# An FFT-mixing kernel's first batch: filter loads held back behind the input, a constant moved to another DMA queue, and filter rows loaded instead of copied

## The chip, the cores and the metric

One core of a Trainium2 chip. The metric is the time of one execution on the device in microseconds (us), lower is better. The kernel before was at 780.32 us (median of three runs, 779.61 to 780.56). The profile's own span leaves out a little at the ends: 778.8 us for that kernel.

## The reference, cut to what matters

```python
# x: (8, 3008, 256); filt_r, filt_i: (1505, 256); w_in: (256, 2048); w_out: (2048, 256)
X = np.fft.rfft(x, axis=1)
F = (filt_r + 1j * filt_i)[None, :, :]
y = np.fft.irfft(X * F, n=3008, axis=1).astype(np.float32)
t = y.reshape(24064, 256)
h = t @ w_in
out = np.maximum(0.01 * h, h) @ w_out
```

The FFT of length 3008 = 94 x 32 is done as matmuls with constant matrices: `small` (the first, 94-point step, and the last, 32-point step of the inverse), `f2` (the second step with its twiddles) and `i1` (the inverse). Between the steps, transposes and products with the filters run on the vector engine.

## The kernel before

Batches 1 to 7 are mixed while the two big matmuls of the batches before them keep TensorE busy. Batch 0 has nothing to hide behind, so it has its own, quicker code, and nothing of the big matmuls starts before it is through. It is done in two halves of 128 channels ("first half", "second half"). The filter tiles `fa_sb` and `fb_sb` need the same rows twice: in partitions 0 to 63 (loaded from DRAM) and again in 64 to 127 ("upper rows", copied).

The loads, as they are issued at the top. All but `small` go through the queue that GpSimd issues to:

```python
def filt_load(dst, src, d0, dn):          # two loads of 192 KB, fp32 in DRAM, fp16 in the tile
    for q, first, sgn in ((0, 0, 1), (Q, N1, -1)):
        nc.gpsimd.dma_start(
            dst[q : q + Q, :, ds(d0, dn)],
            bass.AP(tensor=src.tensor, offset=src.offset + first * D + d0,
                    ap=[[N1 * D, N2 // 2], [sgn * NC * D, 2], [sgn * D, NC], [1, dn]]))

nc.sync.dma_start(small_sb[:], small_d.ap())                 # SyncE's queue
first_parts = ((0, 10), (10, 10), (20, 8), (28, 4))
for n0, nn in first_parts:
    x_load(0, n0, nn)                                        # batch 0 in four parts
for hf in range(2):
    filt_load(fa_sb, filt_r, hf * DH, DH)
    filt_load(fb_sb, filt_i, hf * DH, DH)
    for i in (1, 0, 2) if hf == 0 else ():
        nc.gpsimd.dma_start(f2_sb[:, ts(i, NC // FP), :], f2_d.ap()[i])
nc.gpsimd.dma_start(w_in_sb[:], moe_w_in.rearrange("(dt p) c -> p dt c", p=P))
```

The work of batch 0:

```python
def upper(hf, t, copy):
    copy(t[64:P, :, ts(hf, DH)], t[0:64, :, ts(hf, DH)])

keep_warm(14)                       # matmuls on zeros, to have TensorE at full clock
g = 0
for n0, nn in first_parts:
    while nn:
        n = 2 if nn % 4 or n0 >= N2 - 4 else 4
        first_s1(n0, n, two[n // 4], (dve, act)[g % 2])     # 94-point step, result copied to big
        n0, nn, g = n0 + n, nn - n, g + 1
    keep_warm(5 if n0 < N2 else 14)
t1_part(0, 0, True)(), t1_part(0, 1, True)()                # transposes, first half
upper(0, fa_sb, act), upper(0, fb_sb, dve)                  # upper rows of the first half
first_s2(0, 8, 8, "ph", True)                               # matmuls with f2, products with fa, fb
t1_part(0, 2, True)()
first_s2(0, 0, 8, "ph")

nc.vector.memset(i1_sb[:, 0, 0:2], 0.0)                     # the i1 load waits for this memset
nc.sync.dma_start(i1_sb[:], i1_d.ap())
for n0 in (0, N2 // 2):
    x_load(1, n0, N2 // 2)
t1_part(0, 3, True)()
upper(1, fa_sb, act)                                        # upper rows of the second half
first_s2(0, 16, 4, "pf"), first_s2(0, 20, 4, "pf")
upper(1, fb_sb, dve)
keep_warm(4)
first_s2(1, 0, 8, "ph")
# ... rest of batch 0, then the steady loop over the big matmuls
```

A small memset in front of a load is the kernel's way of holding the load back: the load overwrites what the memset wrote, so it waits for the memset, which stands behind other work in the vector engine's order.

Of the kernel before, what the change touches and what calls it, by code (L numbers as in the profile page):

```python
# [10 lines left out]
P = 128  # L11
# [7 lines left out]
N1, N2 = 94, 32  # L19
NC = 24  # L20
Q = 32
R1 = 96
FP = 3
# [46 lines left out]
def kernel(  # L70
# [9 lines left out]
    nc = tc.nc  # L80
    B, N, D = x.shape
# [11 lines left out]
    f2_d = nc.inline_tensor(f2_np, name="fwd2_const")  # L93
    i1_d = nc.inline_tensor(i1_np, name="inv1_const")
    small_d = nc.inline_tensor(small_np, name="small_const")

    cpool = ctx.enter_context(tc.tile_pool(name="const", bufs=1))
    f2_sb = cpool.tile([P, NC, P], FP16, name="f2_sb")
    i1_sb = cpool.tile([P, N2, N1], FP16, name="i1_sb")
    small_sb = cpool.tile([P, 3, P], FP16, name="small_sb")  # L100
    fa_sb = cpool.tile([P, NC, D], FP16, name="fa_sb")
    fb_sb = cpool.tile([P, NC, D], FP16, name="fb_sb")
    w_in_sb = cpool.tile([P, NDT, DFF], FP16, name="w_in_sb")
    w_out_sb = cpool.tile([P, NCT, D], FP16, name="w_out_sb")
    x_sb = cpool.tile([P, N2, D], FP16, name="x_sb")
# [15 lines left out]
    def bank(kind, n, w):  # L121
        of = wide if kind == "ph" else single
        t = of[turn[kind] % len(of)]
        turn[kind] += 1
        return t[:, : n * w].rearrange("p (n w) -> p n w", n=n)
# [4 lines left out]

    DH = D // 2

    def x_load(b, n0=0, nn=N2, d0=0, dn=D):

        for lo, cnt in ((0, R1),) if b + 1 < B else ((0, 64), (64, N1 - 64)):
            nc.gpsimd.dma_start(  # L136
                x_sb[lo : lo + cnt, ds(n0, nn), ds(d0, dn)],
                bass.AP(tensor=x.tensor, offset=x.offset + (b * N + lo * N2 + n0) * D + d0,
                        ap=[[N2 * D, cnt], [D, nn], [1, dn]]))

    def filt_load(dst, src, d0, dn):

        for q, first, sgn in ((0, 0, 1), (Q, N1, -1)):
            nc.gpsimd.dma_start(
                dst[q : q + Q, :, ds(d0, dn)],
                bass.AP(tensor=src.tensor, offset=src.offset + first * D + d0,
                        ap=[[N1 * D, N2 // 2], [sgn * NC * D, 2], [sgn * D, NC], [1, dn]]))


    nc.sync.dma_start(small_sb[:], small_d.ap())  # L150
    first_parts = ((0, 10), (10, 10), (20, 8), (28, 4))
    for n0, nn in first_parts:
        x_load(0, n0, nn)
    for hf in range(2):
        filt_load(fa_sb, filt_r, hf * DH, DH)
        filt_load(fb_sb, filt_i, hf * DH, DH)
        for i in (1, 0, 2) if hf == 0 else ():
            nc.gpsimd.dma_start(f2_sb[:, ts(i, NC // FP), :], f2_d.ap()[i])
    nc.gpsimd.dma_start(w_in_sb[:], moe_w_in.rearrange("(dt p) c -> p dt c", p=P))
    idle = cpool.tile([P, CH], FP16, name="idle")  # L160
    nc.vector.memset(idle[:], 0.0)

# [18 lines left out]
    def spread(dst, n0, ps, copy, e0=0):  # L181
        nn, de = ps.shape[1], ps.shape[2] // 2
        copy(paired(dst)[:, ds(n0, nn), ds(e0, de)], ps.rearrange("p n (e t) -> p n e t", t=2))  # L183
# [3 lines left out]
    def t1_part(b, i, flat=False):  # L187
        def go():
            a = big[(4 * b) % 3][:].bitcast(FP32)[:, ts(i, E4 * Q)].rearrange("p (e n) -> p e n", n=Q)
            o = big[(4 * b + 1) % 3][:].bitcast(FP32)  # L190
            if flat:
                o = o[:, ts(i, E4 * Q)].rearrange("p (e n) -> p e n", n=Q)
            else:
                o = o.rearrange("p (n e) -> p e n", n=Q)[:, ts(i, E4), :]
            nc.vector.transpose(o, a)  # L195
        return go
# [52 lines left out]
    act, dve = nc.scalar.copy, nc.vector.tensor_copy  # L249

    def first_s1(n0, n, kind, copy):
        ps = bank(kind, n, D)
        for j in range(0, n, 2):
            nc.tensor.matmul(ps[:, ds(j, 2), :], fwd1[:N1], x_sb[:N1, ds(n0 + j, 2), :],  # L254
                             start=True, stop=True)
        spread(big[0], n0, ps, copy)
# [50 lines left out]
        yv = yt[:, dt, :N].rearrange("p (a c) -> p a c", c=N2)  # L307
        copy(yv[:, :, ds(4 * h, 4)], ps.rearrange("p c a -> p a c"))

    def upper(hf, t, copy):  # L310
        copy(t[64:P, :, ts(hf, DH)], t[0:64, :, ts(hf, DH)])


    def keep_warm(n):
        for _ in range(n):
            nc.tensor.matmul(po_ps.rearrange("p a d -> p (a d)"), idle[:, 0:P], idle[:],  # L316
                             start=True, stop=True)

    keep_warm(14)
    g = 0  # L320
    for n0, nn in first_parts:
        while nn:
            n = 2 if nn % 4 or n0 >= N2 - 4 else 4
            first_s1(n0, n, two[n // 4], (dve, act)[g % 2])
            n0, nn, g = n0 + n, nn - n, g + 1
        keep_warm(5 if n0 < N2 else 14)
    t1_part(0, 0, True)(), t1_part(0, 1, True)()
    upper(0, fa_sb, act), upper(0, fb_sb, dve)
    first_s2(0, 8, 8, "ph", True)
    t1_part(0, 2, True)()  # L330
    first_s2(0, 0, 8, "ph")

    nc.vector.memset(i1_sb[:, 0, 0:2], 0.0)
    nc.sync.dma_start(i1_sb[:], i1_d.ap())
    for n0 in (0, N2 // 2):
        x_load(1, n0, N2 // 2)
    t1_part(0, 3, True)()
    upper(1, fa_sb, act)
    first_s2(0, 16, 4, "pf"), first_s2(0, 20, 4, "pf")
    upper(1, fb_sb, dve)  # L340
    keep_warm(4)
    first_s2(1, 0, 8, "ph")
    first_sa(0, 0, 8)
# [87 lines left out]
    for slot in range(SL * (NCHUNK + 1)):  # L431
        ci, g = divmod(slot, SL)
# [36 lines left out]
```

## Time and profile before

| | before |
|---|---|
| device time, median of 3 | 780.32 us |
| span in the profile | 778.8 us |
| TensorE busy | 768.5 us |
| x's first matmul | 7.07 us |
| first transposes of batch 0 on the vector engine | 14.77 us |
| first matmul of the second half | 22.87 us |
| first matmul of the steady loop (L377) | 39.36 us |

TensorE is busy nearly throughout, so the steady loop cannot give or take much; whatever moves the first matmul of L377 moves the end. The prediction below shows the chain of waits and the loads. Two more lines of the timeline of the kernel before belong to its argument (start in us, duration, engine, line, operation, operands, count; in brackets the idle time of the engine just before, and what ended it):

```profile
22.87 1.04 PE L267 MATMUL ph<-big,f_sb 128*128 128x128 f16 x8 [2.01 <-DVE big L195]
...
39.36 1.31 PE L377 MATMUL ph<-yt,w_in_sb 128*128 128x512 f16 x4
```

The first says that TensorE stands still for 2.01 us in front of the second half, because the transpose of L195 on the vector engine is what it waits for. The second is the marker: all before it is front, all after it is the steady loop.

### The profile page before, as it was taken

The numbers are of one execution on the slowest core, as the hardware profiler recorded it, in microseconds if no ns is written. First come the engines' busy times: TensorE is split into PE (matmuls) and PEld (weight loads), VectorE is DVE, ScalarE is ACT, GpSimd is POOL, SyncE is SP. The second block draws the span as 40 slices with busy tenths as digits, with TensorE's granted clock in tenths as the row PEclk, the third lists the DMA queues.
The fourth block names the chain that finished last, engine by engine and source line by source line (L and its number), as shares of the span: only waits on it lengthen the run. The fifth ranks groups of instructions, "written<-read, shape, count | busy, mean of one in ns | idle before, by whom it ended". The sixth has DMA issues, their size and how long they took to land.

```text
span 778.8 us, 13329 instructions
## 1 busy us (share of the span) xinstructions
PE 768.5 (99%) x5688; PEld 521.5 (67%) x5688; DVE 369.6 (47%) x468; ACT 553.5 (71%) x784; POOL 148.7 (19%) x123
## 2 busy tenths in 40 slices
PE   8899999999999999999999999999999999999998
PEld 4556666666776676666777667666667667666666
DVE  5989742765238641576407743187523764200000
ACT  5777768676787768777686775967668676666663
POOL 6854200330005200042002410025000330000000
PEclk9999999999999999999999999999999999999999
DMA  9951013210151010510105010230101010110111
GB/s 186 227 92 56 28 41 71 66 42 29 41 108 42 28 41 28 116 35 28 42 28 122 28 41 29 53 96 28 41 28 42 28 38 31 41 42 28 41 41 55
DMA packets 36154, 43.36 MB, mean 56 GB/s; under 512 B 8130, under 2 KB 34370, under 8 KB 35330
## 3 DMA queue, kind: packets, MB, share of 16 engines
q0 software_dynamic: 10208, 17.01, 12.4%
q1 hardware_dynamic: 25888, 25.52, 9.3%
q8 instruction: 44, 0.72, 0.4%
q14 instruction: 14, 0.11, 0.1%
HBM read 34.10 MB, written 24.64 MB: 75 GB/s over the span
## 4 chain that ended last, share of the span: by engine, by line
PE 96%; DVE 2%; ACT 1%; DMA 1%; issue 0%; DVEq 0%; POOLq 0%
PE ph L377 41%; PE po_ps L391 41%; PE pf L173 3%; PE pf L241 2%; PE pf L213 2%; PE pf L229 2%; PE pf L391 1%; DMA x_sb<-in_x_dram 1%; DVE big L195 1%; DVE prod L281 1%; PE pf L288 0%; ACT big L183 0%; PE po_ps L316 0%; PE ph L267 0%; PE ph L254 0%
## 5 line engine op out<-in xcount | busy, mean ns | idle before, releaser
L382 ACT ACTIVATE gt_c<-ph 128x1024 f16<-128x1024 f32 x376 | 384.9, 1024 | 195.5 <-PE ph L377 193.4
L377 PE MATMUL ph<-yt,w_in_sb 128*128 128x512 f16 (+3 forms) x1600 | 386.6, 367 | 0.3
L391 PE MATMUL po_ps<-w_out_sb,gt_c 128*128 128x256 f16 x2944 | 381.5, 273 | 0.5 <-ACT ost_c_t L398 0.5
L391 PEld LDWEIGHTS <-gt_c 128*128 128x128 f16 x3008 | 290.5, 98 | 82.3 <-issue 2.4
L377 PEld LDWEIGHTS <-w_in_sb 128*128 128x128 f16 x1600 | 154.4, 98 | 97.5 <-issue 0.4
L222 POOL TENSOR_TENSOR y_b_g<-p_b_g,p_b_g 128x512 f16<-128x512 f32 x84 | 106.8, 1272 | 225.7 <-DVE p_b_g L220 225.7
L195 DVE STREAM_TRANSPOSE big<-big 128x1024 f32<-128x1024 f32 x32 | 56.0, 1846 | 126.0 <-ACT big L183 125.9
L183 ACT CAST big<-pf 128x512 f16<-128x512 f32 x186 | 106.6, 605 | 1.1 <-PE pf L254 1.1
L244 DVE CAST yt<-pf 128x376 f16<-128x376 f32 x112 | 56.4, 545 | 86.0 <-PE pf L241 86.0
L218 DVE TENSOR_TENSOR p_b_g<-pf,fa_sb 128x512 f32<-128x512 f32 x84 | 58.1, 692 | 38.3 <-PE pf L213 35.3
L398 ACT COPY ost_c_t<-po_ps 128x256 f32<-128x256 f32 x184 | 69.4, 377 | 6.6 <-PE po_ps L391 5.4
L203 DVE STREAM_TRANSPOSE big<-big 128x1024 f32<-128x1024 f32 x28 | 51.1, 1936 | 34.0 <-ACT big L183 34.0
L219 DVE TENSOR_TENSOR p_b_g<-pf,fb_sb 64x512 f32<-64x512 f32 x84 | 58.2, 692 | 1.1
L220 DVE TENSOR_TENSOR p_b_g<-pf,fb_sb 64x512 f32<-64x512 f32 x84 | 57.4, 683 | 1.1
L136 POOL DMA_DIRECT2D x_sb<-in_x_dram x13 | 7.1, 548 | 253.7 <-PE pf L173 252.9
L241 PEld LDWEIGHTS <-big 128*128 128x128 f16 x448 | 25.7, 98 | 13.2
L173 PE MATMUL pf<-x_sb,small_sb 94*128 94x512 f16 x112 | 33.6, 380 | 0.2 <-DVE yt L244 0.2
L213 PE MATMUL pf<-big,f_sb 128*128 128x256 f16 x168 | 32.1, 273 | 0.0
L229 PE MATMUL pf<-y_b_g,small_sb 128*128 128x512 f16 x84 | 31.9, 380 | 0.0
L213 PEld LDWEIGHTS <-f_sb 128*128 128x128 f16 x168 | 16.4, 98 | 19.7
L241 PE MATMUL pf<-i_sb,big 128*128 128x94 f16 x448 | 28.7, 206 | 0.0
L173 PEld LDWEIGHTS <-small_sb 94*128 94x128 f16 x112 | 10.7, 98 | 10.5
(50 smaller groups left out, 166.8 us busy)
## 6 DMA issues: line engine op xcount, KB each, us to landing
out_dram<-ost_c_t SPq DMA_DIRECT2D x92, 256.0 KB, 2.1
x_sb<-in_x_dram POOLq DMA_DIRECT2D x5, 1536.0 KB, 11.1
x_sb<-in_x_dram POOLq DMA_DIRECT2D x2, 768.0 KB, 12.1
x_sb<-in_x_dram POOLq DMA_DIRECT2D x3, 480.0 KB, 7.3
w_in_sb<-in_moe_w_in_dram POOLq DMA_DIRECT2D x1, 1024.0 KB, 13.3
w_out_sb<-in_moe_w_out_dram POOLq DMA_DIRECT2D x1, 1024.0 KB, 11.8
x_sb<-in_x_dram POOLq DMA_DIRECT2D x1, 1024.0 KB, 8.1
fa_sb<-in_filt_r_dram POOLq DMA_DIRECT2D x4, 192.0 KB, 8.5
```

The costliest lines, as they stand in the source:

```text
L173: nc.tensor.matmul(ps, fwd1[:N1], x_sb[:N1, ds(2 * g, 2), :], start=True, stop=True)
L183: copy(paired(dst)[:, ds(n0, nn), ds(e0, de)], ps.rearrange("p n (e t) -> p n e t", t=2))
L195: nc.vector.transpose(o, a)
L213: nc.tensor.matmul(ps[:, j, :], f2_sb[:, 2 * g + j, :], src[:, 2 * g + j, :], start=True, stop=True)
L218: nc.vector.tensor_tensor(p1[:], ps, fa, AL.mult)
L219: nc.vector.tensor_tensor(p2[0:64], ps[64:P], fb[64:P], AL.mult)
L222: nc.gpsimd.tensor_tensor(y1[:], p1[:], p2[:], AL.add)
L241: nc.tensor.matmul(ps[:, j, :], src[:, dt, n2, :], i1_sb[:, n2, :], start=True, stop=True)
L377: nc.tensor.matmul(ph[:, j, ds(o, ln)], w_in_sb[:, dt, ts(ct, P)], yt[:, dt, ds(lo, ln)], start=(dt == 0), stop=(dt == NDT - 1),)
L382: nc.scalar.activation(gts[ci][:, ds(2 * g, 2), :], ph, AF.Lrelu)
L391: nc.tensor.matmul(po, gts[ci][:, ct, ts(tj, P)], w_out_sb[:, ct, :], start=(ct == 0), stop=(ct == NCT - 1))
L398: nc.scalar.copy(ost[:, tj % 2, :], po)
```

## The change

The intent, as the code shows it: let x come in alone, with the filters held until the first copies of batch 0 are done; take `f2` and most of `small` to SyncE's queue, held a little longer; fetch the upper rows of the second half from DRAM, which takes a copy each from ScalarE and the vector engine; and load `w_in` later. Ten warming matmuls instead of 14 stand in front, as if x were expected earlier.

```diff
-    nc.sync.dma_start(small_sb[:], small_d.ap())
+    nc.sync.dma_start(small_sb[:, 0, :], small_d.ap()[:, 0, :])
     first_parts = ((0, 10), (10, 10), (20, 8), (28, 4))
     for n0, nn in first_parts:
         x_load(0, n0, nn)
-    for hf in range(2):
-        filt_load(fa_sb, filt_r, hf * DH, DH)
-        filt_load(fb_sb, filt_i, hf * DH, DH)
-        for i in (1, 0, 2) if hf == 0 else ():
-            nc.gpsimd.dma_start(f2_sb[:, ts(i, NC // FP), :], f2_d.ap()[i])
-    nc.gpsimd.dma_start(w_in_sb[:], moe_w_in.rearrange("(dt p) c -> p dt c", p=P))
 # ... filt_load gets an argument p0, the first partition to write
-    keep_warm(14)
+    keep_warm(10)
 # ...
             first_s1(n0, n, two[n // 4], (dve, act)[g % 2])
+            if g == 0:
+                nc.vector.memset(fa_sb[0:1, 0, 0:2], 0.0)
+                for hf in range(2):
+                    filt_load(fa_sb, filt_r, hf * DH, DH)
+                    filt_load(fb_sb, filt_i, hf * DH, DH)
+                filt_load(fa_sb, filt_r, DH, DH, 64)
+                filt_load(fb_sb, filt_i, DH, DH, 64)
+            if g == 2:
+                nc.vector.memset(f2_sb[:, 8, 0:2], 0.0)
+                for i in (1, 0, 2):
+                    nc.sync.dma_start(f2_sb[:, ts(i, NC // FP), :], f2_d.ap()[i])
+                nc.sync.dma_start(small_sb[:, 1:3, :], small_d.ap()[:, 1:3, :])
 # ...
     nc.sync.dma_start(i1_sb[:], i1_d.ap())
+    nc.gpsimd.dma_start(w_in_sb[:], moe_w_in.rearrange("(dt p) c -> p dt c", p=P))
 # ...
-    upper(1, fa_sb, act)
     first_s2(0, 16, 4, "pf"), first_s2(0, 20, 4, "pf")
-    upper(1, fb_sb, dve)
```

More of the change, by code (lines that the diff above doesn't have):

```diff
@@ L131, with x_load, filt_load @@
     DH = D // 2
-    def x_load(b, n0=0, nn=N2, d0=0, dn=D):
+    def x_load(b, n0=0, nn=N2):
         for lo, cnt in ((0, R1),) if b + 1 < B else ((0, 64), (64, N1 - 64)):
             nc.gpsimd.dma_start(
-                x_sb[lo : lo + cnt, ds(n0, nn), ds(d0, dn)],
-                bass.AP(tensor=x.tensor, offset=x.offset + (b * N + lo * N2 + n0) * D + d0,
-                        ap=[[N2 * D, cnt], [D, nn], [1, dn]]))
-    def filt_load(dst, src, d0, dn):
-        for q, first, sgn in ((0, 0, 1), (Q, N1, -1)):
+                x_sb[lo : lo + cnt, ds(n0, nn), :],
+                bass.AP(tensor=x.tensor, offset=x.offset + (b * N + lo * N2 + n0) * D,
+                        ap=[[N2 * D, cnt], [D, nn], [1, D]]))
+    def filt_load(dst, src, d0, dn, p0=0):
+        for q, first, sgn in ((p0, 0, 1), (p0 + Q, N1, -1)):
             nc.gpsimd.dma_start(
@@ L308, in first_sb, with upper @@
         copy(yv[:, :, ds(4 * h, 4)], ps.rearrange("p c a -> p a c"))
-    def upper(hf, t, copy):
-        copy(t[64:P, :, ts(hf, DH)], t[0:64, :, ts(hf, DH)])
+    def upper(t, copy):
+        copy(t[64:P, :, :DH], t[0:64, :, :DH])
     def keep_warm(n):
@@ L327 @@
     t1_part(0, 0, True)(), t1_part(0, 1, True)()
-    upper(0, fa_sb, act), upper(0, fb_sb, dve)
+    upper(fa_sb, act), upper(fb_sb, dve)
     first_s2(0, 8, 8, "ph", True)
```

## The prediction

> **What bounds the kernel now.** I read the page first: PE is busy 768.5 of 778.8 us, and in the chain that ended last PE has 96%. So the kernel is TensorE-bound wherever its steady loop runs. The diff touches nothing in that loop; it touches only the first batch, before the first matmul of L377. I therefore asked for the timeline, which puts that matmul at 39.36 us, and for the chain cut to the first 45 us. A microsecond won or lost ahead of 39 us is a microsecond of the total, because PE has no slack afterwards to absorb it; nothing else in the change can reach the end.
>
> The chain of the first 45 us, in order of time (start, length, what):
>
> ```profile
> 1.24 5.78 DMA x_sb<-in_x_dram
> 8.31 1.08 PE po_ps L316 x5
> 14.07 0.67 ACT big L183
> 14.77 2.38 DVE big L195 x2
> 18.15 1.25 DVE big L195
> 19.40 2.24 DVE prod L281 x2
> 21.64 1.18 DVE big L195
> 25.95 2.67 PE pf L288 x8
> 29.16 2.48 DVE prod L281 x4
> 31.65 2.29 DVE big L296 x2
> ```
>
> The reader is to see three things. The chain enters x's first transfer once, then goes through PE with its warming matmuls (L316) until x is in. From 14.77 to about 22.8 it is the vector engine that sets the pace. The two upper copies of the second half, L311 at 20.86 on ACT and 25.21 on DVE, are not long pieces of it: in the second case PE is, since 8 matmuls of L288 took 2.67 us there.
>
> The timeline then says who waited for what (start, length, engine, line, in brackets the idle time before and its releaser):
>
> ```profile
> 12.38 0.74 POOL L144 DMA_DIRECT2D fa_sb<-in_filt_r_dram  x1 [0.45 <-DMA x_sb<-in_x_dram]
> 14.76 2.75 ACT L311 COPY fa_sb<-fa_sb 64x3072 f16<-64x3072 f16 x1
> 16.94 1.33 POOL L159 DMA_DIRECT2D w_in_sb<-in_moe_w_in_dram  x1 [0.56 <-DMA fb_sb<-in_filt_i_dram]
> 17.17 0.95 DVE L311 COPY fb_sb<-fb_sb 64x3072 f16<-64x3072 f16 x1
> 17.18 2.52 PEld L267 LDWEIGHTS <-f_sb 128*128 128x128 f16 x24 [0.62 <-DMA f_sb<-fwd_const]
> 20.86 2.75 ACT L311 COPY fa_sb<-fa_sb 64x3072 f16<-64x3072 f16 x1 [1.52 <-DMA fa_sb<-in_filt_r_dram]
> 25.21 0.95 DVE L311 COPY fb_sb<-fb_sb 64x3072 f16<-64x3072 f16 x1
> ```
>
> The kernel's GpSimd loads take eight completion semaphores in turn, so a load waits for the one eight before it. The first line's wait is thus for x's fourth part: it landed at about 12.1 us (0.3 us from landing to issue, as elsewhere). The third line's is for the first half's last filter load: about 16.6. Its reader, the DVE copy, started at 17.17, right behind two transposes. The slack of this load is only 0.5 us.
>
> Last, what the DMA engines moved (by microsecond: TensorE clock, DMA share, GB/s at the end of a row):
>
> ```profile
> 10.00:11.00 1.00, 1.00 (x6) 0.43 (x5) 0.78 (x1) 0.72 (x2) 0.10 (x1) 1.00 1.09 195
> 12.00:13.00 1.00, 1.00 (x6) 0.41 (x5) 0.87 (x1) 0.44 (x1) 0.62 (x1) 1.00 1.82 180
> 16.00:17.00 1.00, 1.00 (x5) 0.29 (x3) 1.00 (x2) 1.00 (x1) 0.44 (x2) 1.00 1.03 391
> 26.00:27.00 1.00, 1.00 (x3) 0.30 (x2) 0.97 (x2) 1.00 (x3) 0.35 (x1) 0.50 1.06 304
> ```
>
> x moves at about 200 GB/s until 11 us, then the filters at 180, then f2 at 390, then filters again. The packets in the trace agree: no 256-byte filter packet starts before 11 us, and x's stop there. So the GpSimd queue is first in, first out. The fourth row also shows the TensorE clock at half, after PE had sat idle from 20.9 to 22.9.
>
> **What the Trainium skill says.** "DMA: Bandwidth & Descriptors", section "Queues, rings and completion order": each DMA engine takes turns between the queues it has work for, a packet at a time. The trace agrees: while w_in (GpSimd queue, 4096-byte packets) and i1 (SyncE's queue, 6016-byte packets) both ran at 25.5 to 26.5 us, 16 packets of each started per half microsecond. Same page, "Issuing engines are not separate DMA queues": a load issued from another engine shares the same 16 DMA engines. So f2 moved to SyncE gains no bandwidth, only a turn. Same page, "Specifications": under 512 B a transfer is read-modify-write; the filters' 256-byte packets with 1.82 of share for 180 GB/s agree in being expensive. "TensorE: Matmul & The Clock Gate", "Part 1": the clock is halved by a free-running window of 3413 ns with too little PE work. The trace's half-clock stretch lasted 3.41 us, after a window in which PE was busy about 40%, so agrees.
>
> **The change part by part.**
>
> (a) Filters and f2 held behind the first L183 copies. The purpose is an earlier x. But x had the queue to itself anyway, as it came first. The page gives 11.1 us from issue to landing for later whole x loads with nothing behind; the first batch's four parts, the same 1536 KB, took 12.1 - 1.24 = 10.9. I expect x's first part at 7.0 us, at best 0.3 earlier. The held filters are released by a memset after the DVE copy that ends at 8.17; GpSimd needs about 1.65 us from issue to first packet (as for x: 1.24 to 2.9), so they are ready at 9.9, before x is through at 11.0. Effect: 0.
>
> (b) f2 (768 KB) and two thirds of small (64 KB) go to SyncE's queue, released at about 9.6 behind the third group's copy (8.35 + 1.23). About 1 us later its 2048-byte packets take turns with filter packets of 256 bytes, so they pass nearly at once: 832 KB / 390 GB/s = 2.1 us. Before, f2 ran behind the first half's filters. Now it runs ahead, so these land 2.1 us later: the last of them at 16.6 + 2.1 = 18.7 us, against 17.17 when DVE wants it. DVE stands still for about 1.5 us (1.1 if f2 and filter packets overlap in an engine). What f2 gains is worthless: it lands near 14.5, but its first matmul also needs the transposes that end at 17.15.
>
> (c) Upper rows of the second half: two copies removed, 2.75 us of ACT and 0.95 of DVE; four loads of 192 KB added. At 180 GB/s that is 4 x 1.07 = 4.3 us more DMA. Filters end at 11.0 + 2.1 + 12 x 1.07 = 25.9. i1 (752 KB, 2 us) is released at about 23.2 and cuts in, giving about 28, landing 29.3. The product of fb with the second half would start on DVE at about 26.2 - 0.95 + 1.2 + 1.5 = 28.0, so it waits 1.3 us. But the next DVE products need PE's L267, which I place at 30.8 (29.16 + 1.5 and a little for colder PE), so most of this wait is hidden: 0 to 0.4 us on the path. The 0.95 us of DVE removed is worth little for the same reason: after it DVE waited for PE, 0.61 us before 29.16.
>
> (d) Warming matmuls 14 to 10. Four fewer at 0.22 us let PE end at 4.8 instead of 5.7 and idle 2.3 us until x at 7.07, instead of 1.4. This may halve the clock for one window: some 7 matmuls at 0.43 instead of 0.22, up to 1.5 us on PE. Then the transposes end near 18.6, no later than the filters of (b), so it is not added to (b).
>
> (e) w_in goes from before to behind the filters and the first products: data at about 28 to 33, wanted at 41; the next x by 42, its second half wanted at 46. Both are off the path.
>
> Sum: (a) 0, (b) +1.5, (c) +0.2 with -0.2 back from the copies, (d) 0. PE is also idle longer in front of the second half (20.9 to about 24.4), so more of its next matmuls run at half clock: +0.1 to 0.4. Together about +1.6 us: 780.3 + 1.6 = 781.9.
>
> **Rivals.** First, the intended gain: x comes earlier by a microsecond, as the cut of warming matmuls suggests that its author thought, and the removed copies shorten DVE. For it: DVE is busy nearly throughout from 15 to 32 us. Against: the first-in first-out order above and the same landing time of lone loads. It would make about 779. Second, the wait is hidden: f2 slower than I think on its new queue, or filters overlapping it, so that the last first-half filter lands near 17.3; then only the copies count, and the half-clock stretch could fall elsewhere: 779.5 to 780.5. Third, the added loads bite fully: fb's upper rows land past 30 us, DVE and GpSimd wait for them, and the clock is low twice: about 783.5. Fourth, an upset of the steady loop by later w_in, w_out or x would cost more, but each has 5 us or more of slack.
>
> **Range and chances.** The before runs span 0.95 us alone. I take 781.8, and 779.5 to 783.5 for 8 in 10: the low end holds the second rival, the high end the third. 2% is 15.6 us, more than a third of the whole front of 39 us; nothing here can move that much. Faster 0.01, within 2% 0.98, slower 0.01.
>
> **What would show it.** In the profile after: x's first matmul at 7.0 +- 0.3 (a); DVE's fb copy waiting for a filter DMA until 18.2 to 19, and f2 no longer a releaser (b); a DVE or GpSimd wait for a fb load near 28 to 29 (c); a half-clock stretch near 7.5 to 11 us in some runs (d); the first L377 matmul at 40.5 to 41.3 instead of 39.36, and from there to the end the same time as before (739.4 us). I am wrong if x's first matmul comes before 6.5, if the fb copy starts by 17.4, or if the stretch after the first L377 differs by over 1 us.

## The result, and the profile after

The changed kernel took 784.17 us (median of four runs, 783.66 to 785.34) against 780.03 us for the kernel before (four runs), a ratio of 1.0055 with a 95% interval of 1.0037 to 1.0072. Ratios here are the mean time of one kernel's fast runs over the mean of the other's in the same rounds, so they are not quite the ratio of the medians quoted. All experiments gave correct results. So it is slower, by 4.1 us (0.55%, still within 2%) and not by the 1.6 predicted, and outside the predicted range. Line numbers shift by 6: L377 is now L383, L267 is L261, L195 is L189, L281 is L275, L311 is L305.

The profiled run was the slowest of the four (785.34 us, span 783.6), so its gap of 4.8 us is a little more than the median's. The chain of waits over its first 50 us (start, length, what):

```profile
1.24 5.51 DMA x_sb<-in_x_dram
...
10.34 10.89 DMA fb_sb<-in_filt_i_dram
...
22.31 1.14 DVE big L189
...
23.48 2.32 DVE prod L275 x2
...
30.64 2.76 PE pf L282 x8
...
36.43 2.29 DVE big L290 x2
```

One piece is new and long: from 10.34 to 21.23 us the end depends on a load of `fb`. Before, PE, ScalarE and the vector engine filled that stretch. The timeline shows who stood still for it:

```profile
9.35 1.28 SPq L330 DMA_DIRECT2D f_sb<-fwd_const  x3
...
14.49 2.37 DVE L189 STREAM_TRANSPOSE big<-big 128x1024 f32<-128x1024 f32 x2 [0.21 <-ACT big L177]
...
19.11 2.75 ACT L305 COPY fa_sb<-fa_sb 64x3072 f16<-64x3072 f16 x1 [4.65 <-DMA fa_sb<-in_filt_r_dram]
...
21.32 0.95 DVE L305 COPY fb_sb<-fb_sb 64x3072 f16<-64x3072 f16 x1 [4.46 <-DMA fb_sb<-in_filt_i_dram]
...
27.02 1.04 PE L261 MATMUL ph<-big,f_sb 128*128 128x128 f16 x8 [6.43 <-DVE big L189]
...
44.15 1.30 PE L383 MATMUL ph<-yt,w_in_sb 128*128 128x512 f16 x4
```

The vector engine's copy of the first half's upper `fb` rows started at 21.32 instead of 17.17, after 4.46 us of waiting for the load of `fb`. TensorE's gap in front of the second half grew from 2.01 to 6.43 us. The loss can be followed from marker to marker:

| marker | before | after | difference so far |
|---|---|---|---|
| x's first matmul | 7.07 | 6.80 | -0.27 |
| first transposes | 14.77 | 14.49 | -0.28 |
| `fb` copy, first half | 17.17 | 21.32 | +4.15 |
| first matmul of the second half | 22.87 | 27.02 | +4.15 |
| transposes of the inverse (in the chain: L296, L290) | 31.65 | 36.43 | +4.78 |
| first matmul of the steady loop | 39.36 | 44.15 | +4.79 |
| end of the span | 778.8 | 783.6 | +4.8 |

So x came 0.27 us earlier, the stall at the `fb` copy cost 4.43, and the second half took 0.63 longer. After that nothing changed: 739.4 us from the marker to the end in both.

What happened to the load is seen in what the DMA engines moved. The view of busy time by stretches, kernel after (last three columns: TensorE clock, DMA share, GB/s):

```profile
12.00:13.00 1.00, 1.00 (x7) 0.43 (x5) 1.00 (x1) 0.71 (x1) 1.00 (x2) 1.00 1.32 240
...
14.00:15.00 1.00, 1.00 (x6) 0.48 (x5) 0.79 (x2) 0.46 (x1) 0.00 (x0) 1.00 1.41 257
...
18.00:19.00 1.00, 1.00 (x12) 1.00 (x11) 0.00 (x0) 0.00 (x0) 0.42 (x1) 1.00 1.82 180
...
24.00:25.00 1.00, 0.00 (x0) 0.00 (x0) 1.00 (x2) 0.00 (x0) 1.00 (x2) 0.50 1.82 180
...
30.00:31.00 1.00, 1.00 (x8) 0.73 (x7) 1.00 (x2) 0.73 (x2) 0.00 (x0) 0.50 0.87 184
```

Before, the engines ran filters at 180 GB/s and then `f2` at 390. Now they run a mixture at 240 to 283 GB/s from 12 to 16 us, and filters alone again from 17. The last two rows show TensorE's clock at one half, which lasted from 22.4 to 32.6 us, three windows of 3.41 us instead of one. This goes with the 0.63, but was not isolated. From the first matmul of the second half to the marker, e12 below took 15.9 us with no such window, the kernel before 16.5 with one, the change 17.1 with three; yet e5 and e8, both with two, took 16.7 and 17.2.

The trace also has a record of each packet and of the moment at which each of the 16 DMA engines reports its share of a load as done. The last of the 16 reports of the first half's last filter load decides when the `fb` copy may start. In microseconds of the span, for the kernel before, one in which `f2` runs whole ahead of the filters in the same queue, and those that cross `f2` with the filters:

```text
                        x's last part   first half's last filter load        fb copy
                        (median         (median      (last        (last -    starts
                         engine)         engine)      engine)      median)
before                    11.29           15.81        16.66        0.85      17.17 (did not wait)
f2 ahead, one queue       11.23           17.76        18.31        0.55      18.40
f2 moved, no hold         11.32           17.91        18.56        0.65      18.65
change without hold       11.37           18.24        18.87        0.63      18.96
f2 moved, and hold        11.28           18.03        20.15        2.12      20.24
f2 in long rows, hold     11.23           18.09        19.61        1.52      19.70
change, 14 warming        11.29           18.69        21.29        2.60      21.38
change                    11.23           18.51        21.23        2.72      21.32
change (second look)      11.18           19.09        20.46        1.37      20.55
```

In every row but the first, the copy starts 0.09 us after the last engine's report (in the second row the transposes ahead of it end at that moment too, so it shows no wait). The Trainium skill has the reason on the page "DMA: Bandwidth & Descriptors", section "Why a DMA increments its semaphore by 16 and not by 1": only when all 16 engines have counted is the whole load known to have landed. This column of last reports is what the prediction should have estimated; the experiments below take it apart.

### The profile page after: what moved, and what is told of

Its sections match the earlier page's. It is cut to its first block, busy times and chain, and to the rows that moved or that the text cites. A ratio compares the mean times of both kernels' runs of the same rounds, so it can differ in the third digit from the quotient of the medians.

```text
span 783.6 us, 13332 instructions
## 1 busy us (share of the span) xinstructions
PE 768.9 (98%) x5684; PEld 521.8 (67%) x5684; DVE 368.6 (47%) x469; ACT 551.2 (70%) x783; POOL 149.7 (19%) x124
## 4 chain that ended last, share of the span: by engine, by line
PE 94%; DMA 2%; DVE 1%; ACT 1%; issue 0%; POOL 0%; DVEq 0%; POOLq 0%
PE ph L383 41%; PE po_ps L397 41%; PE pf L167 3%; PE pf L235 2%; PE pf L207 2%; PE pf L223 2%; DMA fb_sb<-in_filt_i_dram 1%; PE pf L397 1%; DMA x_sb<-in_x_dram 1%; DVE prod L275 1%; PE pf L282 1%; ACT big L177 0%; DVE big L189 0%; DVE big L290 0%; PE ph L299 0%
## 5 line engine op out<-in xcount | busy, mean ns | idle before, releaser
L383 PE MATMUL ph<-yt,w_in_sb 128*128 128x512 f16 (+3 forms) x1600 | 386.4, 366 | 0.3
L383 PEld LDWEIGHTS <-w_in_sb 128*128 128x128 f16 x1600 | 154.5, 98 | 97.4 <-issue 0.4
L189 DVE STREAM_TRANSPOSE big<-big 128x1024 f32<-128x1024 f32 x32 | 56.0, 1846 | 126.0 <-ACT big L177 125.9
L207 PE MATMUL pf<-big,f_sb 128*128 128x256 f16 x168 | 32.1, 273 | 0.0
## 6 DMA issues: line engine op xcount, KB each, us to landing
w_out_sb<-in_moe_w_out_dram POOLq DMA_DIRECT2D x1, 1024.0 KB, 14.6
```

What stands on the lines that cost most here:

```text
L207: nc.tensor.matmul(ps[:, j, :], f2_sb[:, 2 * g + j, :], src[:, 2 * g + j, :], start=True, stop=True)
L383: nc.tensor.matmul(ph[:, j, ds(o, ln)], w_in_sb[:, dt, ts(ct, P)], yt[:, dt, ds(lo, ln)], start=(dt == 0), stop=(dt == NDT - 1),)
```

## The experiments

Two sizes were to be explained: the load that came 4.6 us later instead of 2.1, and a total of 4.1 us instead of 1.6. The main theory was the prediction's: `f2` crossing the filters makes them late, and everything else is worth about nothing. Its rivals put the rest down to the hold of the filters, to the four loads of upper rows, or to the smaller number of warming matmuls. Each text says what the theories of its moment expected. Edits are against the changed kernel ("change") or against the kernel before ("before"), as named.

| kernel | median us | before, same rounds | ratio (95% interval) |
|---|---|---|---|
| e1 change again | 784.39 | 780.48 | 1.0054 (1.0039-1.0069) |
| e2 f2 behind the filters, GpSimd queue | 783.02 | 780.48 | 1.0039 (1.0021-1.0057) |
| e3 f2 ahead of them, GpSimd queue | 781.69 | 780.48 | 1.0016 (1.0001-1.0031) |
| e4 before, only f2 moved | 781.73 | 780.48 | 1.0018 (1.0003-1.0033) |
| e5 change, 14 warming matmuls | 784.02 | 780.36 | 1.0049 (1.0034-1.0064) |
| e6 e2 with 14 | 785.46 | 780.36 | 1.0063 (1.0048-1.0078) |
| e7 e4 with the hold | 784.16 | 780.36 | 1.0051 (1.0036-1.0066) |
| e8 e5 without the hold | 782.69 | 780.36 | 1.0029 (1.0013-1.0046) |
| e9 before, only upper rows loaded | 783.41 | 780.61 | 1.0033 (1.0021-1.0046) |
| e10 one queue | 780.56 | 780.61 | 1.0000 (0.9987-1.0014) |
| e11 e10, TensorE warmed in the gap | 780.43 | 780.61 | 1.0005 (0.9992-1.0017) |
| e12 before, TensorE warmed in the gap | 779.82 | 780.61 | 0.9990 (0.9978-1.0003) |
| e13 change, f2 in long rows | 783.23 | 780.45 | 1.0038 (1.0025-1.0051) |
| e14 e11 with wide filter rows | 783.76 | 780.45 | 1.0045 (1.0033-1.0058) |
| e15 e12 with wide filter rows | 783.89 | 780.45 | 1.0048 (1.0034-1.0061) |

### e1: the change again

No edit.

> The changed kernel once more, unaltered, beside the runs below. Theory (f2 on its own queue ahead of the first half's filters): again 783.5 to 785.5 us, with DVE's fb copy waiting for a filter load until about 21 us, and of the 16 DMA engines one or two reporting that load over 1 us after the rest. Rival (the straggling engine was an accident of the one profiled execution): the load lands near 19.7, where 15 of the 16 engines had reported it, DVE starts its copy there, and the profile's span is about 782.

784.39 us (784.10 to 785.61): the result repeats. Its profile came by the same time in another way:

```profile
17.66 2.37 DVE L189 STREAM_TRANSPOSE big<-big 128x1024 f32<-128x1024 f32 x2 [0.21 <-ACT big L177]
...
20.55 0.95 DVE L305 COPY fb_sb<-fb_sb 64x3072 f16<-64x3072 f16 x1 [0.52 <-DMA fb_sb<-in_filt_i_dram]
```

Here the clock was at half until 13.4 us, so the transposes came 3.2 us later than in the first profile; yet the `fb` copy came even a little earlier, and waited for the load all the same. TensorE's lateness hides in the load's. That is two profiles of one kernel, so the chain of one profile should not be taken for the kernel's.

### e2 and e6: f2 behind the first half's filters, in GpSimd's queue

```diff
+                    if hf == 0:                # inside the held block, after the first half's filters
+                        for i in (1, 0, 2):
+                            nc.gpsimd.dma_start(f2_sb[:, ts(i, NC // FP), :], f2_d.ap()[i])
-                nc.vector.memset(f2_sb[:, 8, 0:2], 0.0)
-                for i in (1, 0, 2):
-                    nc.sync.dma_start(f2_sb[:, ts(i, NC // FP), :], f2_d.ap()[i])
+                nc.vector.memset(small_sb[:, 1, 0:2], 0.0)
 # e6 also: keep_warm(10) -> keep_warm(14)
```

> The changed kernel with one thing undone: f2 goes back to the GpSimd queue, behind the first half's filters; the held loads, the upper rows from DRAM and 10 warming matmuls stay. Theory (f2's new place is the cause): the first half's last filter lands near 16.7, DVE's fb copy starts near 17.0, first matmul of the steady loop at 38.5 to 39.7, total 779.3 to 780.7. Rival A (the hold behind the first copies is the cause): stays at 783 to 785. Rival B (the four extra loads are the cause): fb copy near 17.0 but a wait in the second half, total 782 to 784.

> Run e2 (f2 back behind the first half's filters on the GpSimd queue, rest as changed) with 14 warming matmuls. e2 had two levels, 781.6 and 784.4, though its filters were in time. Theory (that is the cold clock alone): transposes at 14.5 to 14.7, fb copy at 16.9 to 17.2, one level, total 779.0 to 780.3. Rival (holding the loads or the added loads cost something too): above 781.

e2 fell into two groups: 781.50 and 781.72, 784.31 and 784.43. The profile is of the first (781.50). In it the copy no longer waits:

```profile
18.21 0.95 DVE L305 COPY fb_sb<-fb_sb 64x3072 f16<-64x3072 f16 x1
```

With `f2` behind them the filters are in time (last report 16.57), and the copy follows directly on transposes that began at 15.80; 10 warming matmuls had brought the full clock only at 9.8 us, so here their number does show. That the first half is restored by taking `f2` out of the filters' way speaks for the prediction's mechanism.

e6 was to remove the cold start too, and got slower, 785.46 (784.18 to 785.63). Its chain of waits:

```profile
10.06 8.18 DMA fb_sb<-in_filt_i_dram
...
21.02 11.06 DMA fb_sb<-in_filt_i_dram
...
32.16 1.24 DVE prod L275
```

Two loads of `fb` set the pace. In the first half only `small`'s 64 KB crossed the filters, and one engine came 2.2 us behind the median (18.24 against 16.08), a second 1.6 us. In the second half `i1`, on SyncE's queue, crossed the loads of upper rows: the last two engines reported their last load at 30.2 and 32.1, the other 14 by 27.9, and the vector engine waited 4.1 us. So a crossing can cost much even where few bytes cross. It need not: in e2, with the same loads and the same hold, `small`'s packets began at 13.4 us instead of 11.6, and the last engine was only 0.3 us behind the median. The slow group of e2 was not profiled; that it is this collision is likely and not shown.

### e3: f2 ahead of the filters, in GpSimd's queue

```diff
+                for i in (1, 0, 2):            # ahead of the held filters
+                    nc.gpsimd.dma_start(f2_sb[:, ts(i, NC // FP), :], f2_d.ap()[i])
-                nc.vector.memset(f2_sb[:, 8, 0:2], 0.0)
-                for i in (1, 0, 2):
-                    nc.sync.dma_start(f2_sb[:, ts(i, NC // FP), :], f2_d.ap()[i])
+                nc.vector.memset(small_sb[:, 1, 0:2], 0.0)
```

> The changed kernel with f2 on the GpSimd queue but ahead of all filters: same bytes in the same order of need, but one queue, no turns between queues. Theory (two thirds of the loss is lost in taking turns and in an engine left behind by it): the filters are late by f2's bare 2.0 us, last one at 18.7 to 19.0, as the prediction had it, DVE's copy there, total 781.3 to 782.6. Rival (being behind f2 at all costs 4 us, the queues don't matter): 783.5 to 785.

781.69 us (781.66 to 781.80), the steadiest of the held kernels.

```profile
18.40 0.95 DVE L305 COPY fb_sb<-fb_sb 64x3072 f16<-64x3072 f16 x1
```

The copy shows no wait, but only because the transposes ahead of it, late from the cold start (15.99), end at 18.36; the load's last report came at 18.31. (The memset is on `fa_sb`, so `f2` itself was not held: it was issued at 3.45, right behind x's parts.) This is the prediction's arithmetic without any crossing: 768 KB put ahead of the filters make their median report 6.53 us behind x's instead of 4.52, so 2.0 us later, which is what 768 KB at 390 GB/s come to, and the last engine is 0.55 us behind the median. So `f2`'s bytes ahead of the filters explain 2 us of delay, and the change has 4.6: the rest needs more than these bytes.

### e4: the kernel before, with f2 alone moved

```diff
-        for i in (1, 0, 2) if hf == 0 else ():
-            nc.gpsimd.dma_start(f2_sb[:, ts(i, NC // FP), :], f2_d.ap()[i])
 # ...
             first_s1(n0, n, two[n // 4], (dve, act)[g % 2])
+            if g == 2:
+                nc.vector.memset(f2_sb[:, 8, 0:2], 0.0)
+                for i in (1, 0, 2):
+                    nc.sync.dma_start(f2_sb[:, ts(i, NC // FP), :], f2_d.ap()[i])
```

> The kernel before with one part of the change alone: f2 on SyncE's queue, released behind the third group's copy; filters issued at once, copies of the upper rows as before, 14 warming matmuls. Theory: this alone makes the loss, fb copy at 20 to 21.5, total 783 to 785. Rival A or B (hold, or extra loads): near 780.

781.73 us (781.57 to 782.24).

```profile
18.65 0.95 DVE L309 COPY fb_sb<-fb_sb 64x3072 f16<-64x3072 f16 x1 [1.65 <-DMA fb_sb<-in_filt_i_dram]
```

This is the prediction's step (b) by itself, and it comes out as the prediction had it: a wait of 1.65 us (1.5 predicted), last filter report at 18.56 (18.7 predicted), total +1.4 by the ratio (+1.6 predicted for the whole change). The step was right about a kernel that was not the one asked about. Both theories for this run missed (783 to 785, or near 780): the second queue by itself cost no more than running `f2` ahead in one queue (781.69 in e3). By-finding: the three loads were issued at 9.57, but no packet of theirs ran before 13.37. Then 20 packets started within 0.25 us, and the last at 16.6.

### e5: the change with 14 warming matmuls

```diff
-    keep_warm(10)
+    keep_warm(14)
```

> The changed kernel with 14 warming matmuls again. In three of the last four profiles (all with 10) the TensorE clock reached full speed only at 10.1 to 13.7 us and the transposes began 1.2 to 2.9 us late. Theory 1 (in the whole change the late filters hide the cold clock): transposes begin near 14.6, but DVE's fb copy still waits for its load until 20 to 21.5; total 783.3 to 784.7, as the change. Theory 2 (the cold clock is a main part of the loss): total 781 to 782.5.

784.02 us (783.61 to 784.95), the change's time.

```profile
21.38 0.95 DVE L305 COPY fb_sb<-fb_sb 64x3072 f16<-64x3072 f16 x1 [4.61 <-DMA fb_sb<-in_filt_i_dram]
```

So the fewer warming matmuls are not the cause. With the clock at full before x arrives, the copy waits 4.61 us (4.46 in the change's first profile, where that was so too, 0.52 in e1) for a load that is as late as ever.

### e7: e4 with the hold of the filters; e8: the whole change without it

```diff
 # e7, against e4 (w_in stays behind the filters, inside the held block)
-    for hf in range(2):                        # at the top
-        filt_load(fa_sb, filt_r, hf * DH, DH)
-        filt_load(fb_sb, filt_i, hf * DH, DH)
+            if g == 0:                         # in the first_s1 loop
+                nc.vector.memset(fa_sb[0:1, 0, 0:2], 0.0)
+                for hf in range(2):
+                    filt_load(fa_sb, filt_r, hf * DH, DH)
+                    filt_load(fb_sb, filt_i, hf * DH, DH)
 # e8, against e5: the held block without its memset, back at the top
```

> The kernel before with f2 on SyncE's queue (as e4, which lost 1.2 us with fb copy at 18.65) and the filters held behind the first copy as well; copies of upper rows, 14 warming matmuls as before. Theory (a hold puts the filters' issue just ahead of f2's, and the two queues then share badly on some engines): f2's packets start on the engines at different times, the load's last engine reports near 20.5 to 21.3, total 783 to 785. Rival (the hold is harmless, the rest of the loss beyond e4 comes from the four added loads): fb copy near 18.7, total 781.3 to 782.2.

> The changed kernel with the filters issued at once again, behind x, and 14 warming matmuls; f2 and the rest of small on SyncE's queue, upper rows from DRAM. Theory (the hold makes the difference between e4 and the change): fb copy at 18.5 to 19, total 781.0 to 782.2. Rival (the added loads do, as they keep GpSimd's queue full and GpSimd writing descriptors): fb copy at 20 to 21.3, total 783 to 785.

e7 took 784.16 us (783.44 to 785.22), e8 782.69 (782.38 to 783.06). The copy in e7, then in e8:

```profile
20.24 0.95 DVE L305 COPY fb_sb<-fb_sb 64x3072 f16<-64x3072 f16 x1 [3.19 <-DMA fb_sb<-in_filt_i_dram]
```

```profile
18.96 0.95 DVE L310 COPY fb_sb<-fb_sb 64x3072 f16<-64x3072 f16 x1 [1.89 <-DMA fb_sb<-in_filt_i_dram]
```

The two point the same way. Taking the hold out of the change (e5 to e8) makes the copy 2.4 us earlier and the median 1.3 us shorter; putting it into e4 (e7) makes the copy 1.6 us later and the median 2.4 us longer. Part of the difference between the two lies in profiled runs at different ends of their spread (e5's was its slowest, e7's its fastest). So the hold, which the prediction put at zero, is the larger part of what it missed. And e7, `f2` moved and the filters held, is by itself as slow as the whole change (784.16 against 784.17), with neither added loads nor fewer warming matmuls.

How it acts is in the table of reports. The median engine moves little with the hold: from 17.91 to 18.03 with `f2` alone (e4, e7), from 18.24 in e8 to 18.51, 18.69 and 19.09 in the three profiles of the change. What grows more, but for the last of these, is the lag of the last engine behind the median, from 0.6 to between 1.4 and 2.7 us in all held kernels that cross `f2` with the filters. In the packet records, `f2`'s packets start at about 13.4 in the kernels without the hold and take 3.2 us, with about as many packets of `f2` as of filters per half microsecond (68 and 71 in the one about 14.0, e4). The engines keep level: they report `f2`'s first load between 14.6 and 15.2 (e4). With the hold the packets start at 11.5 to 13.1. In the change about 40 of `f2` and 150 of filters then start per half microsecond, it takes 5.9 us (11.5 to 17.4) until the last has started, and the reports of `f2`'s first load are spread from 12.8 to 16.0. Why the engines keep level in the one case and fall apart in the other, no run shows: the start of SyncE's packets, right behind x or two microseconds later, goes with it, but was not varied by itself. It does order the kernels better than the hold does: in held kernels whose SyncE packets begin at 11.5 to 11.9 us the lag is 1.5 to 2.7 us (change, e5, e6, e7, e13); where they begin at 13.1 to 13.9 it is 1.4, 0.3 and 0.55 (e1, e2, e3), and without the hold, at 13.4, it is 0.6.

e8 is still 1.0 us over e4 (782.69 against 781.73; other rounds, before at 780.36 and 780.48). Its copy is 0.31 us later, probably as `small`'s 64 KB cross too, and its clock stays at half for two windows (23.6 to 30.4) where e4 has one.

### e9: the kernel before, with only the second half's upper rows loaded

```diff
+    filt_load(fa_sb, filt_r, DH, DH, 64)       # at the top, ahead of w_in
+    filt_load(fb_sb, filt_i, DH, DH, 64)
 # ...
-    upper(1, fa_sb, act)
-    upper(1, fb_sb, dve)
```

> The kernel before with part (c) alone: four loads for the second half's upper rows behind the other filters in place of the two copies; f2 on the GpSimd queue, nothing held, 14 warming matmuls. Theory (a SyncE load that meets the filters' queue is what costs): first half untouched, fb copy near 17.1; but i1, issued by SyncE near 21.7, now meets the last filter loads, so fb's upper rows are in on the last engine only at 28 to 31 us and DVE or GpSimd waits for them: total 780.5 to 783. Rival (the added loads are harmless and the saved copies pay): 779.0 to 780.0.

783.41 us (782.06 to 783.57; the profile is of the fastest). The first half is as before (copy at 16.93). Then the vector engine's product with `fb` in the second half waits:

```profile
29.75 1.23 DVE L283 TENSOR_TENSOR prod<-ph,fb_sb 128x1024 f16<-128x1024 f32 x1 [3.68 <-DMA fb_sb<-in_filt_i_dram]
```

`i1` crosses the tail of these loads at 25 to 28 us, and their last engine reports near 29.7. So part (c) alone costs 2.6 us by the ratio. In the whole change this wait is absent: the stall in the first half has already pushed the product to 30.39 us, and the rows are in by about 30.2. The parts are not additive: repairing (b) alone would have exposed (c), as e6 shows.

### e10 to e12: no crossings, and TensorE warmed in the gap

e10 is the repaired form of the change: everything in GpSimd's queue in the order x, first half's filters, `f2`, second half's filters, upper rows; `i1` and `w_in` behind them; 14 warming matmuls. e11 is e10, and e12 the kernel before, with 12 instead of 4 warming matmuls in TensorE's gap.

```diff
 # e10, against before
+    filt_load(fa_sb, filt_r, DH, DH, 64)       # after both halves' filters
+    filt_load(fb_sb, filt_i, DH, DH, 64)
-    nc.gpsimd.dma_start(w_in_sb[:], ...)       # w_in goes behind i1
-    nc.vector.memset(i1_sb[:, 0, 0:2], 0.0)
-    nc.sync.dma_start(i1_sb[:], i1_d.ap())
+    nc.gpsimd.dma_start(i1_sb[:], i1_d.ap())
+    nc.gpsimd.dma_start(w_in_sb[:], ...)
-    upper(1, fa_sb, act)
-    upper(1, fb_sb, dve)
 # e11 (on e10) and e12 (on before)
-    keep_warm(4)
+    keep_warm(12)
```

> All large loads on the GpSimd queue, in the order of need: x, first half's filters, f2, second half's lower and upper rows, i1, w_in; small whole at the start on SyncE, nothing held, 14 warming matmuls, upper rows of the second half from DRAM. Theory (without meetings of the two queues there is no straggling engine): fb copy near 17.1, fb's upper rows on the last engine by 27.3, no wait for them or less than 1 us, total 779.5 to 780.6, about the kernel before. Rival (the 768 KB more of loads costs in any case): over 781.

> e10 with 12 instead of 4 warming matmuls in front of the second half, so that PE isn't idle for 2 us there. Theory (the half-clock stretch near 24 us costs 0.6 to 1 us and hides the two saved copies): 0.6 to 1.3 us under e10, 778.4 to 779.6, faster than the kernel before. Rival (DVE and the late filters bound that stretch): no better than e10.

> The kernel before with nothing changed but 12 instead of 4 warming matmuls in front of the second half. Theory (the spread of the kernel before, 779.6 to 780.8 with mean clocks of 1.000 and 0.997 to 0.998, is the half-clock stretch that some executions have): all runs at the fast end, 779.3 to 779.9. Rival: no change.

e10 took 780.56 us, ratio 1.0000. The longest wait that the copies' removal leaves:

```profile
27.00 1.22 DVE L282 TENSOR_TENSOR prod<-ph,fb_sb 128x1024 f16<-128x1024 f32 x1 [0.75 <-issue]
```

The view says "issue", but the wait ends 0.08 us after the last engine's report of `fb`'s upper rows (26.92), so it is this load. It does no harm, as the vector engine's next product waits for TensorE in any case (29.11 here, 29.16 before). So with nothing crossing, loading the upper rows costs nothing, and the two removed copies (2.75 us of ScalarE, 0.95 of the vector engine) bring nothing. e11 took 780.43 us, with two of five runs near 782; its profile has new vector-engine waits of 0.69 and 0.83 us in the second half, the second for the upper `fb` rows, so TensorE's gain runs into the rows' arrival.

e12, the kernel before with the gap filled, took 779.82 (779.55 to 780.22). Its timeline and one stretch:

```profile
23.04 1.04 PE L267 MATMUL ph<-big,f_sb 128*128 128x128 f16 x8 [0.28 <-DVE big L195]
```

```profile
24.00:25.00 1.00, 1.00 (x8) 0.52 (x7) 1.00 (x3) 0.46 (x1) 0.68 (x2) 1.00 1.06 213
```

TensorE's gap shrinks from 2.01 to 0.28 us, the half-clock stretch is gone, and the median is 0.8 us below that of the same rounds. It is the only kernel here that may beat the kernel before, but its interval (0.9978 to 1.0003) touches 1, so the gain is not shown.

### e13: the change with f2 in one load of long rows

If `f2`'s many short turns beside the filters make them late, a few long ones should not.

```diff
-    fwd2 = fwd2.reshape(P, FP, NC // FP, P).transpose(1, 0, 2, 3)
-                for i in (1, 0, 2):
-                    nc.sync.dma_start(f2_sb[:, ts(i, NC // FP), :], f2_d.ap()[i])
+                nc.sync.dma_start(f2_sb[:], f2_d.ap())
 # and keep_warm(14)
```

> The changed kernel with 14 warming matmuls (as e5, 784.0) and one difference: f2 is one load of 128 rows of 6144 bytes on SyncE's queue in place of three loads with rows of 2048. Theory P (turns by packet): a third as many turns, f2 is through in about 2.5 us, the first half's last filter is in near 18.7 to 19.3, total 781.5 to 782.7. Theory Q (any meeting of the queues leaves an engine behind): the last engine reports near 21, total 783.3 to 785.

783.23 us (782.09 to 784.33), between what the two theories said.

```profile
19.70 0.95 DVE L304 COPY fb_sb<-fb_sb 64x3072 f16<-64x3072 f16 x1 [2.71 <-DMA fb_sb<-in_filt_i_dram]
```

Against e5 the copy is 1.7 us earlier. The packets of 6144 bytes took 248 ns each, 128 of them, so 1.98 us per engine; the change's 384 packets of 2048 bytes at 96 ns take 2.30. The median engine's report came 0.6 us earlier for it. The last engine is still 1.5 us behind, mostly one engine: the other 15 had reported by 18.45. So the number of turns explains part of the delay, and the lag of one engine with the hold remains.

### e14 and e15: filter rows at their whole width

Both load filter rows of 256 channels at once instead of 128, e14 in the order of e11, e15 in that of e12, with `f2` behind both filters. In the packet records the rows that run backwards in DRAM became packets of 512 bytes (1536 of them), and those that run forwards were joined to packets of 12288 bytes (64).

```diff
-    for hf in range(2):
-        filt_load(fa_sb, filt_r, hf * DH, DH)
-        filt_load(fb_sb, filt_i, hf * DH, DH)
-        for i in (1, 0, 2) if hf == 0 else ():
-            nc.gpsimd.dma_start(f2_sb[:, ts(i, NC // FP), :], f2_d.ap()[i])
+    filt_load(fa_sb, filt_r, 0, D)
+    filt_load(fb_sb, filt_i, 0, D)
+    for i in (1, 0, 2):
+        nc.gpsimd.dma_start(f2_sb[:, ts(i, NC // FP), :], f2_d.ap()[i])
```

> e11 (one queue, 12 warming matmuls in front of the second half; it lost about 1.5 us waiting for the upper rows) with the lower filter rows loaded in whole width: four loads of 384 KB with rows of 512 bytes in place of eight of 192 KB with rows of 256. If the 256-byte packets are what makes the filters slow (180 GB/s against 390 for f2), all lower rows are in by 16.7 as the first half was, the upper rows by 23, no wait for them: total 778.3 to 779.4, faster than the kernel before by 1.2 to 2.2. If the rate doesn't depend on the row, the first half is late by 4 us: 783 to 785.

> e12 (the kernel before with 12 warming matmuls in front of the second half, 779.8) with the lower filter rows in whole width, copies of the upper rows kept. If the filters' rate doubles: the first half's filters are in by 16.7 as before, the second half's 4 us earlier; the copies of upper rows on ACT may begin earlier, but nothing on the path: 779.3 to 780.0, and e14's gain over it is what the saved copies are worth.

783.76 and 783.89 us: both lose. The copy of e14:

```profile
19.99 0.95 DVE L311 COPY fb_sb<-fb_sb 64x3072 f16<-64x3072 f16 x1 [2.90 <-DMA fb_sb<-in_filt_i_dram]
```

A load of 384 KB lands every 1.9 us, of either packet size, about 200 GB/s, hardly better than 180, so the first half waits for twice the bytes. The filters' rate is not limited by their short rows, as the prediction's reading of their 256-byte packets suggested. x, whose packets are of 2048 to 5120 bytes, moves at 200 GB/s too, and `f2` at 390; x and the filters are converted from fp32 on the way (so 360 to 400 GB/s are read for 180 to 200 written), `f2` is not. Packets of 4096 bytes took 324 ns where they were converted (x, `w_in`) and about 168 where not (`f2`). That the conversion or the reads set the limit is likely; no run here separates the two.

## Why the prediction was right or wrong

**Direction right, size wrong:** predicted +1.6 us (781.8), measured +4.1 (784.17), and outside 779.5 to 783.5.

**(a) Right for x, wrong for the hold.** x's first matmul came at 6.80 against 7.07: within 7.0 +- 0.3 and worth nothing, as x had the queue to itself anyway (without any hold it came at 6.82 and 6.75 in e9 and e11). But "Effect: 0" was said of the hold as a whole. It was valued by what it does to x alone; what it does to the meeting of the filters with `f2` was not asked. e7 and e8 put it at 1.3 to 2.4 us.

**(b) The mechanism right, the term mis-sized; this is the step that failed.** As the prediction put it: "so they pass nearly at once: 832 KB / 390 GB/s = 2.1 us [...] these land 2.1 us later: the last of them at 16.6 + 2.1 = 18.7 us [...] DVE stands still for about 1.5 us". Measured: last report at 21.23 instead of 16.66, a wait of 4.46 us. By the table of reports, the shift of 4.57 us is made of three terms:

- x 0.06 earlier.
- From x's last part to the median engine's report, 7.28 instead of 4.52 us: +2.76. This is what the 2.1 stood for. The rate of 390 GB/s had been read from `f2` in GpSimd's queue, where its packets were of 4096 bytes at about 168 ns. On SyncE's queue they are of 2048 bytes, as the prediction expected, at 96 ns, and `small`'s are 128 of 512 bytes at 39: (384 x 96 + 128 x 39) / 16 = 2.6 us per engine. But this sum is 0.2 to 0.3 over what the kernels without the hold show (2.3 against 2.07 in e4, 2.6 against 2.35 in e8), so about 0.4 of the 2.76 goes with the hold.
- The last engine 2.72 behind the median instead of 0.85: +1.87. The prediction had no such term; it reckoned with rates of all engines together, and a load is through only when its slowest engine is. This is the larger part of what comes with the hold: the lag is 0.65 in e4, 0.63 in e8. How the shift falls on the two terms differs from run to run: in e1, the same kernel, they were +3.39 and +0.52.

Without the hold (e4) the step's figures hold to 0.2 us, and with `f2` ahead in the same queue (e3) the 2.1 is measured as 2.0.

**(c) Right in the whole change, wrong by itself.** No wait for upper rows shows, as (b)'s stall covers it, and the copies were worth nothing (e10: 780.56 against 780.61). But the "0 to 0.4 us on the path" was 2.6 where (b) was not there (e9): the third rival, hidden behind the main effect.

**(d) Right in its sum, not in its working.** The missing four warming matmuls are hidden behind the late filters (e5). But TensorE was done with ten at 5.54 us, not at 4.8: they ran at half clock, 0.43 us each instead of 0.22, so it then idled 1.26 us and not 2.3. In the first profile the clock was full from 5.3 us; in e1 only from 13.4, and the total was the same.

**The colder second half:** predicted 0.1 to 0.4 us, measured 0.63, with TensorE idle for 6.43 us instead of the 3.5 expected and the clock at half for 10.2 us instead of 3.41.

**(e) Right.** 739.4 us from the first steady matmul to the end, before and after.

**Two readings** were a little off without consequence: 35 filter packets had started before 11 us, the first at 10.80, while x's last started at 11.59; and x's first packet came at 2.64 us, not 2.9, so 1.4 us after its issue.

**Of the rivals,** the intended gain and the hidden wait did not occur. The figure of the third (783.5) is near the result, though by another mechanism than the one it named.

**What stays open:** why one or two of the 16 DMA engines fall up to 2.7 us behind when SyncE's packets meet the filters early, with the hold, and not when they meet them at 13.4 us without it.

## What to carry to other kernels

A load counts when the slowest of its 16 DMA engines is done, so before a transfer is moved to a second queue, look at what will run in the first one at that moment, and at whose reader has the least slack: here 0.5 us. Putting loads in one queue in the order in which they are wanted cost nothing (e10); letting `f2` or `i1` from a second queue meet loads that were wanted at once cost 1.2 to 5 us (one queue in the wrong order, e3, cost 1.2 too), and the sum of the parts tried alone was not the whole. Take rates from the same queue and packet size that the moved load will have.

## What the Trainium skill lacked or had wrong

- "DMA: Bandwidth & Descriptors", "Queues, rings and completion order": turns between queues are taken a packet at a time, a packet being several descriptors. The prediction read a packet as one record of the trace. Records of `f2` and filters started 68 to 71 in the half microsecond about 14 us in e4, but about 40 to 150 in the change: the page gives no way to tell which mixture will come.
- The same section does not say that engines can drift apart where queues meet: for the first half's last filter load, the last of 16 engines was 1.4 to 2.7 us behind the median in held kernels in which `f2` crossed the filters, and 2.2 in e6, where only 64 KB did, against 0.3 to 1.1 us in all others. Under "Latency and other measured facts" the page has two engines that are usually slower, but no size, and nothing on queues that meet; the traces here do not say which engine a report is from.
- No page has that a SyncE load's first packets may come long after its issue: 9.57 to 13.37 us in e4 and 9.35 to 11.5 in the change, with GpSimd's queue busy in both.
- No page has that the same rows went in packets of 4096 bytes (about 168 ns) from GpSimd's queue and of 2048 bytes (96 ns) from SyncE's.
- The same page, "Specifications": 512 bytes as the least for line rate. Filter loads went from 180 to only about 200 GB/s when their packets grew from 256 to 512 and 12288 bytes (e14, e15), so these loads, which convert fp32 to fp16, were held by something else.
- "TensorE: Matmul & The Clock Gate", "Why this matters for your kernels": it advises against idle gaps of over about 3 us. A gap of 2.01 us was enough here to bring 3.41 us of half clock (before), and filling it (e12) removed that.
